# Splitting the keys of the second layer's first two query units, with the first halves issued beside the last GLU block

## The chip, the cores and the metric

The kernel runs on one core of a Trainium2 chip (trn2). The metric is the device time of one execution in microseconds (us). Before the change the median of three executions is 2244.06 us (2243.4 to 2244.54). One further execution was taken with the profiler; all rows below come from it.

## What is computed

Two identical layers are applied to `x` of 2048 rows and 448 columns. Each is multi-query attention (16 heads of 28, one shared key and value head) followed by a gated block with 1792 hidden columns, both on layer-normed input and added to `x`:

```python
q = (x @ wq).reshape(B, S, H, Dh)          # 16 heads of 28
k, v = x @ wk, x @ wv                      # one head for all
p = softmax(einsum("bhqd,bkd->bhqk", q, k) * Dh ** -0.5)
x = x + einsum("bhqk,bkd->bhqd", p, v).reshape(B, S, H * Dh) @ wo    # on layernorm(x)
x = x + (sigmoid(x @ w_gate) * (x @ w_up)) @ w_down                   # on layernorm(x)
x = the same two lines once more, with the same weights
```

## The kernel before

The program is written out by hand in one order for all engines (`manual_schedule`); every engine works through its own instructions strictly in that order, and what reaches a buffer or a result too early waits.

**Units and steps.** The 2048 query rows are 16 units of 128 rows, the 2048 keys 16 tiles of 128. A step is one unit with one key tile: four score products `s` (line 584, four heads each, 512 columns), four exponentials `P` on ScalarE (line 587), and four products with the values, `pv` (line 595, 32 columns of the array each; the trace shows two records for each, so 8 a step), which sum over the unit's 16 steps into one PSUM tile. A layer is 256 steps. `pv` runs one or two steps behind the scores, from the list `waiting`.

**Row maxima.** The exponential needs each row's maximum first. For each unit and each range of 512 keys, class `Maxima` issues groups of four products `mx` (line 549), which VectorE reduces with four instructions `mp` (line 554). The last quarter of the keys of unit 0 in layer 2 is cut finer (256, 128, 128), since those keys come last. When a unit's groups are done, `row_max` reduces them to one number per row, `fin` transposes it (`mt`, line 575), VectorE copies it (`mr`), and a DMA from GpSimd writes it as row 28 of the unit's queries `QS`, where the score product subtracts it. Only then may the unit's scores start.

**Filler.** Query projections (`qp`, line 352), the output projection (`wo`, line 695) and the gated block (`gp`, `up`, line 352; `dn`, line 784) of units that are done are cut into slices and issued between the scores (`PATHS` gives the pattern of a pair of steps, `Filler.slice` the amount). A gated (GLU) block covers two units, and 14 column tiles of 128 in 7 pairs; its tanh `th` and its `h` go through ScalarE and VectorE. `pvs`, `sums`, `rc` and `lb` (lines 599 to 669) divide a unit by its row sums through small DMAs.

**Between the layers.** Layer 2 needs all keys of layer 1's output, so after step 256 of layer 1 a `while` loop (line 1131) issues the rest of layer 1's filler in rounds of 1800 ns, and beside it those maxima of layer 2 (units 0 to 3) whose keys exist. When the last two units' gated block is through, key tiles 14 and 15 are made on the shortest path (`db`, `dct`, `dd`, `det`), unit 0's last maxima follow, and the loop over layer 2's steps starts. Its first three units have pattern `C`; their filler is only the query projections of blocks 1 to 3, the rest of the maxima of units 0 to 3 (`sparse`) and three `wo`, until the first gated block is ready near step 49.

**Buffers.** PSUM has seven tiles in rotation (tag `f`) for `s`, `mx` and all filler, and one for `pv`. A new tile waits for the readers of the tile seven allocations back.

In the text, the *passage* is the part from layer 1's last score to the first transposition of key tile 14 (1108.3 to 1200.5 us), the *closing* from there to layer 2's first score (to 1222.9 us), and the *light stretch* layer 2's units 0 to 2 (to 1350.5 us).

## Time and profile before

| | us |
|---|---|
| median of three executions | 2244.06 |
| profiled execution | 2247.71 |
| its span, first to last instruction | 2245.9 |
| TensorE busy (PE) | 2195.5 (98%) |
| VectorE busy (DVE) | 1643.7 (73%) |
| ScalarE busy (ACT) | 1552.8 (69%) |
| GpSimd busy (POOL) | 335.9 (15%) |

A timeline row gives the start, the time from the first start to the last end, engine, line, operation, tiles, shape and count. TensorE's records overlap, so what a group costs is read from its start to the start of the next row. A number in square brackets is idle time of the engine ahead of the row and what ended it.

### The profile page before, as it was taken

To read this page: it belongs to the slowest core of one execution; us is meant where nothing else is said; L and a number is where in the kernel's file an instruction comes from. 1 tells how busy PE (TensorE), PEld (TensorE's weight loads), DVE (VectorE), ACT (ScalarE), POOL (GpSimd) and SP (SyncE) were. 2 spreads that over 40 slices of the span, in tenths; PEclk is the share of its full clock that TensorE was granted. 3 is DMA by queue.
4 is the path that set the end of the run, shared out by engine and by line. 5 is a ranking of instruction groups with operands and counts; after the bars stand their busy time and mean duration, and the time that the engine had idled before them with its cause. 6 is when DMAs were issued, how large, how long until landed. Compare 5 with 4: busy or idle time off the path is not lost.

```text
span 2245.9 us, 41454 instructions
## 1 busy us (share of the span) xinstructions
PE 2195.5 (98%) x15915; PEld 1030.8 (46%) x15915; DVE 1643.7 (73%) x2905; ACT 1552.8 (69%) x2595; POOL 335.9 (15%) x590
## 2 busy tenths in 40 slices
PE   7998999999999999999999999999999999999999
PEld 3322344444544445454564324445454544445467
DVE  7888888777777787777796557777777777777222
ACT  5698777776667677676614997777676767777741
POOL 5113764101010100101012010000000000000010
PEclk9999999999999999999999999999999999999999
DMA  4333662323313232331441113323231313223233
GB/s 143 106 97 94 197 215 81 106 79 85 112 60 102 64 100 90 97 107 49 119 154 35 36 52 108 80 88 99 67 108 49 100 59 103 76 88 96 75 118 108
DMA packets 203622, 213.28 MB, mean 95 GB/s; under 512 B 135376, under 2 KB 164240, under 8 KB 203424
## 3 DMA queue, kind: packets, MB, share of 16 engines
q1 hardware_dynamic: 198080, 195.78, 29.2%
q0 software_dynamic: 5344, 14.87, 1.9%
q8 instruction: 124, 2.03, 0.4%
q14 instruction: 74, 0.61, 0.1%
HBM read 175.37 MB, written 23.59 MB: 89 GB/s over the span
## 4 chain that ended last, share of the span: by engine, by line
PE 86%; DVE 8%; ACT 2%; issue 1%; DMA 1%; SPq 1%; POOL 0%; DVEq 0%; ACTq 0%; POOLq 0%
PE pv L595 20%; PE s L584 19%; PE up L352 11%; PE dn L784 11%; PE gp L352 11%; PE mx L549 7%; DVE mp L554 6%; PE wo L695 3%; PE qp L352 2%; ACT P L587 1%; DMA wgu<-wgu_d 0%; DMA rq<-in_A_wq_dram 0%; DMA rc<-sums 0%; PE hot L916 0%; DVE sgu L131 0%
## 5 line engine op out<-in xcount | busy, mean ns | idle before, releaser
L587 ACT ACTIVATE P<-s,esc 128x512 f32<-128x512 f32 x2048 | 1297.8, 690 | 474.5 <-PE s L584 462.8
L554 DVE TENSOR_REDUCE mp<-mx 128x1 f32<-128x512 f32 x2048 | 1269.4, 682 | 389.2 <-PE mx L549 385.4
L584 PE MATMUL s<-QS,KK 96*128 96x512 f16 x2048 | 673.8, 381 | 21.3 <-DVE mp L554 14.8
L352 PEld LDWEIGHTS <-wgu 128*128 128x128 f16 x4928 | 467.6, 97 | 182.1 <-issue 42.9
L595 PE MATMUL pv<-P,VV 128*32 128x512 f32 x4096 | 510.7, 602 | 0.0
L352 PE MATMUL gp<-XT,wgu 128*128 128x256 f16 x2464 | 349.2, 272 | 2.4 <-DVE mp L554 1.7
L352 PE MATMUL up<-XT,wgu 128*128 128x256 f16 x2464 | 348.3, 272 | 0.7 <-DVE mp L554 0.7
L784 PE MATMUL dn<-WD,h 128*128 128x448 f16 x1344 | 301.0, 352 | 0.0
L584 PEld LDWEIGHTS <-KK 96*128 96x128 f16 x2048 | 189.7, 97 | 212.5 <-issue 114.5
L595 PEld LDWEIGHTS pv<-P,VV 128*32 128x32 f32 x4096 | 98.7, 108 | 244.6 <-issue 242.6
L549 PE MATMUL mx<-KK,QH 32*128 32x512 f16 x1792 | 185.3, 386 | 3.0 <-DVE mp L554 1.7
L784 PEld LDWEIGHTS <-h 128*128 128x128 f16 x1344 | 126.5, 97 | 129.4 <-issue 14.5
L549 PEld LDWEIGHTS <-QH 32*128 32x128 f16 x1792 | 46.0, 91 | 256.5 <-issue 252.7
L669 POOL TENSOR_TENSOR lb<-pvs,lb 128x512 f32<-128x512 f32 x32 | 41.1, 1284 | 739.1 <-DMA lb<-sums 619.8
L757 ACT ACTIVATE h<-th 128x512 f16<-128x512 f32 x112 | 70.3, 628 | 61.8 <-DVE th L754 61.5
L754 DVE SCALAR_TENSOR_TENSOR th<-th,up 128x512 f32<-128x512 f32 x112 | 76.2, 680 | 48.9 <-PE up L352 42.2
L306 POOL TENSOR_SCALAR rs<-mv 128x1 f32<-128x1 f32 (+1 forms) x50 | 11.2, 225 | 656.6 <-DVE mv L291 573.6
L352 PE MATMUL qp<-XT,WQ 128*128 128x512 f16 x352 | 108.3, 390 | 0.7 <-DVE mp L554 0.4
L746 ACT ACTIVATE th<-gp,gsc 128x512 f32<-128x512 f32 x112 | 76.8, 685 | 32.8 <-PE gp L352 32.6
L758 DVE SCALAR_TENSOR_TENSOR h<-th,h 128x512 f16<-128x512 f32 x112 | 79.9, 713 | 20.8 <-ACT h L757 20.8
L695 PE MATMUL wo<-WO,oT 128*128 128x448 f16 x384 | 89.7, 352 | 0.2 <-ACT P L587 0.2
L352 PEld LDWEIGHTS <-WQ 128*128 128x128 f16 x352 | 32.9, 99 | 54.9 <-issue 28.9
(151 smaller groups left out, 918.1 us busy)
## 6 DMA issues: line engine op xcount, KB each, us to landing
wgu<-wgu_d SPq DMA_DIRECT2D x224, 512.0 KB
QS<-qd SPq DMA_DIRECT2D x384, 32.0 KB
lb<-sums SPq DMA_DIRECT2D x128, 64.0 KB
xr<-in_A_x_dram SPq DMA_DIRECT2D x32, 224.0 KB
qd<-qst POOLq DMA_DIRECT2D x28, 256.0 KB, 2.7
wgu_d<-sgu POOLq DMA_DIRECT2D x14, 512.0 KB, 3.7
x2d<-x SPq DMA_DIRECT2D x16, 224.0 KB
xr<-x2d SPq DMA_DIRECT2D x16, 224.0 KB
```

The costliest lines, as they stand in the source:

```text
L352: nc.tensor.matmul(ps, a, b, start=n == 0, stop=n == 10)
L549: nc.tensor.matmul(ps[h][:, i * w:(i + 1) * w], qh[32 * h:32 * h + 32, g], KK[l][32 * h:32 * h + 32, 1, ka:kz], start=True, stop=True, til ...
L554: nc.vector.tensor_reduce(o, ps[h].rearrange("p (g k) -> p g k", g=n), axis=AX.X, op=OP.max)
L584: nc.tensor.matmul(s, KK[l][0:96, 0, kt * 128:(kt + 1) * 128], QS[l, u][:, g].rearrange("p h n -> p (h n)"), start=True, stop=True)
L587: nc.scalar.activation(p, s, AF.Exp, scale=esc)
L595: nc.tensor.matmul(v[32 * g:32 * g + 32], VV[l][:, kt], P[g], start=kt == 0, stop=kt == KT - 1, tile_position=(0, 32 * g))
L695: nc.tensor.matmul(p, v["oT"][:, a, h * 128:(h + 1) * 128], WO[:, c, h], start=n == 0, stop=n == 11)
L746: defer(lambda: nc.scalar.activation(th, gp.rearrange("p j n -> p (j n)"), AF.Tanh, scale=gsc))
L754: nc.vector.scalar_tensor_tensor(t, th, 1.0, up.rearrange("p j n -> p (j n)"), op0=OP.add, op1=OP.mult)
L757: nc.scalar.activation(h[:, 0], t, AF.Copy, scale=2.0 ** -17)
L758: defer(lambda: nc.vector.scalar_tensor_tensor(h[:, 1], t, 2.0 ** -17, h[:, 0], op0=OP.mult, op1=OP.subtract), 3)
L784: nc.tensor.matmul(p, hs[f // 2][:, a, o:o + 128], WD[:, f, c], start=n == 0, stop=n == 3 * FC - 1)
```

## The change

For units 0 and 1 of layer 2 the keys are taken in two halves of 8 tiles. The first halves have their own maxima (`part` 0) and are issued in the loop between the layers, one score product after the second and the fourth slice of a round (`ahead`), with `pv` two steps behind; 64 score products in all. Their sums are kept in SBUF as `pva`. The layer's own loop starts at step 16 of a new list of steps, with the second halves of units 0 and 1, then unit 2 and so on. The factor between the two maxima, exp of their difference, is made from both rows (`fe`), spread over the partitions by way of DRAM (`fd`, `fb`) and multiplied into `pva` on GpSimd, which also adds `pva` to the second half. Unit 1's last quarter of keys is now cut finer as unit 0's is. For space, `HB` (buffers of `h`) goes from 10 to 8, `s2` from 3 to 2, and `pvs` from 1 to 2. The core of the diff:

```diff
-    TB, WB, HB = 2, 4, 10
+    TB, WB, HB = 2, 4, 8
...
+    CUT = 8
+    def rescale(l, u):
+        if (l, u) in SCB and (l, u) in PVA:
+            nc.gpsimd.tensor_tensor(PVA[l, u], PVA[l, u], SCB.pop((l, u)), op=OP.mult)
+            scaled.add((l, u))
+
+    def halved(l, u):
+        return l == 1 and u < 2
+
+    def segments(l):
+        out = [(u, 0, CUT) for u in range(U) if halved(l, u)]
+        return out + [(u, CUT if halved(l, u) else 0, KT) for u in range(U)]
...
-        ends = [0, 512, 1024, 1536] + ([1792, 1920] if l and u == 0 else []) + [2048]
+        ends = [0, 512, 1024, 1536] + ([1792, 1920] if l and (u == 0 or halved(l, u)) else []) + [2048]
...
         def started(self):
-            return not any(a[0] == 0 for a in self.todo)
+            return not any(a[0] == 0 or halved(self.l, a[0]) for a in self.todo)
...
         def fin():
...
+            if part:
+                f = wk1.tile([16, 128], F32, tag="s2", name="fe", bufs=2)
+                nc.vector.tensor_tensor(f, r, ROW.pop((l, u)), op=OP.subtract)
+                nc.scalar.activation(f, f, AF.Exp, scale=fsc[0:16])
+                nc.sync.dma_start(fd[u % 2], f)
+                v = {}
+
+                def spread():
+                    v["b"] = wk1.tile([128, 512], F32, tag="lb", name="fb", bufs=1)
+                    for g in range(G):
+                        nc.sync.dma_start(v["b"][32 * g:32 * g + 32], fd[u % 2].rearrange("(g h) n -> g (h n)", g=G)[g:g + 1]
+                                          .to_broadcast([32, 512]))
...
+                def scale():
+                    SCB[l, u] = v["b"]
+                    rescale(l, u)
...
+                later((1, spread), (1, scale))
...
-        if kt == KT - 1:
-            o = wk1.tile([128, 512], F32, name="pvs", bufs=1)
+        if kt == z - 1 and z < KT:
+            o = PVA[l, u] = wk1.tile([128, 512], F32, name="pva")
             nc.scalar.copy(o, v)
+            rescale(l, u)
+        elif kt == z - 1:
+            o = wk1.tile([128, 512], F32, name="pvs", bufs=2)
+            nc.scalar.copy(o, v)
+            if a:
+                nc.gpsimd.tensor_tensor(o, o, PVA.pop((l, u)), op=OP.add)
             PVS[l, u] = o
...
+    def ahead(n):
+        for _ in range(n):
+            u, kt, a, z = STEPS[1][sc[0]]
+            if z == KT or ("m", 1, u, 0) not in stored:
+                return
+            if part_p == [] and len(waiting) > 1:
+                pv(*waiting.pop(0))
+            scores(1, u, kt, a, z, len(part_p), part_p)
+            if len(part_p) == G:
+                waiting.append((1, u, kt, a, z, list(part_p)))
+                part_p.clear()
+                sc[0] += 1
...
-            sparse = [i * (3 * KT - 1) // n for i in range(n)]
+            sparse = [sc[0] + i for i in range(4)]
+            sparse += [sc[0] + 5 + i * (3 * KT - 6 - sc[0]) // (n - 4) for i in range(n - 4)]
...
-        for step in range(U * KT):
-            u, kt = divmod(step, KT)
+        for step in range(sc[0] if l else 0, U * KT):
+            u, kt, lo, hi = STEPS[l][step]
...
-            for _ in range(0 if fine else 5):
+            for i in range(0 if fine else 5):
                 fill.slice(VS / 5)
+                if nx and i in (1, 3):
+                    ahead(1)
...
-                    go = n >= 2 and not fine
+                    go = (n >= 2 or halved(l + 1, a[0])) and not fine
```

Counted in the order of the instructions on TensorE, from layer 1's last score to the start of the gated work in layer 2:

| | passage before | passage now | closing before | closing now | light stretch before | light stretch now |
|---|---|---|---|---|---|---|
| `s` | 0 | 64 | 0 | 0 | 192 | 128 |
| steps of `pv` | 2 | 16 | 0 | 0 | 46 | 32 |
| groups of `mx` | 24 | 27 | 3 | 5 | 23 | 18 |
| `gp` and `up` | 436 | 436 | 0 | 0 | 0 | 0 |
| `dn` | 151 | 151 | 17 | 17 | 0 | 0 |
| `qp` | 0 | 0 | 50 | 50 | 78 | 77 |
| `wo` | 12 | 12 | 0 | 0 | 24 | 24 |

From unit 3's first step on, TensorE's order is the same but for one `qp`. Before layer 1's last score one transposition (`mt`) is added, and the maxima of layer 2 that are taken early come in another order.

On ScalarE, in the passage, gated work alone stood in a row before (`th` is the tanh, `h` its use after VectorE's product, `ktl` and `VV` the new keys and values):

```order
L746 ACTIVATE th<-gp,gsc 128x512
L379 ACTIVATE ktl_112<-kv 128x7x28
L380 ACTIVATE VV<-kv 128x28
L757 ACTIVATE h<-th 128x512
L746 ACTIVATE th<-gp,gsc 128x512
```

At the same place it now reads:

```order
L809 ACTIVATE th<-gp,gsc 128x512
L379 ACTIVATE ktl_112<-kv 128x7x28
L380 ACTIVATE VV<-kv 128x28
L641 ACTIVATE P<-s,esc 128x512 x4
L820 ACTIVATE h<-th 128x512
L641 ACTIVATE P<-s,esc 128x512 x2
L809 ACTIVATE th<-gp,gsc 128x512
```

Some six exponentials stand in each pair of `th` and `h`, two of them behind an `h`.

On VectorE, in the closing, after key tile 14 was transposed (`hl` is the last split of the layer norm, `ktl` key tile 15, `m` the row maximum of unit 0), before:

```order
L323 TENSOR_TENSOR hl<-xn,hl 128x384
L554 TENSOR_REDUCE mp<-mx 128x4 x4
L381 SCALAR_TENSOR_TENSOR ktl_112<-kv,ktl_112 128x28
L554 TENSOR_REDUCE mp<-mx 128x4 x4
L569 TENSOR_REDUCE m_16176<-mp 128x16
L570 TENSOR_SCALAR m_16177<-m_16176 128x16
L577 COPY mr<-mt 16x128
```

and now:

```order
L323 TENSOR_TENSOR hl<-xn,hl 128x384
L580 TENSOR_REDUCE mp<-mx 128x4 x8
L381 SCALAR_TENSOR_TENSOR ktl_112<-kv,ktl_112 128x28
L580 TENSOR_REDUCE mp<-mx 128x4 x4
L599 TENSOR_REDUCE m_16595<-mp 128x16
L600 TENSOR_SCALAR m_16596<-m_16595 128x16
L610 COPY mr<-mt 16x128
L614 TENSOR_TENSOR fe<-mr,mra 16x128
L580 TENSOR_REDUCE mp<-mx 128x4 x4
L599 TENSOR_REDUCE m_16632<-mp 128x16
L600 TENSOR_SCALAR m_16633<-m_16632 128x16
```

Four reductions of unit 1 now stand ahead of `ktl`, and four more with their row maximum behind unit 0's.

On TensorE, in the passage, one step's `pv` now stands alone between the gated products:

```order
L352 MATMUL up<-XT_14696,wgu 128x256
L651 MATMUL pv<-P,VV 32x512 x4
L638 LDWEIGHTS KK
L638 MATMUL s<-QS,KK 128x512
L352 LDWEIGHTS wgu
```

In the light stretch they stood, and stand, two steps in a row.

## Rows read from the trace of the kernel before

**Rows 1.** The page: busy time and share of each engine; one group of GpSimd.

```profile
PE 2195.5 (98%) x15915; PEld 1030.8 (46%) x15915; DVE 1643.7 (73%) x2905; ACT 1552.8 (69%) x2595; POOL 335.9 (15%) x590
...
L669 POOL TENSOR_TENSOR lb<-pvs,lb 128x512 f32<-128x512 f32 x32 | 41.1, 1284 | 739.1 <-DMA lb<-sums 619.8
```

**Rows 2.** Busy time by window: passage, closing, light stretch; after the colon the length.

```profile
core 0: us, PE busy (x) PEld busy (x) DVE busy (x) ACT busy (x) POOL busy (x), PEclk, DMA share, GB/s
1108.30:1200.50 92.20, 91.90 (x743) 60.18 (x741) 79.58 (x141) 17.47 (x31) 8.65 (x27) 1.00 0.38 120
1200.50:1222.90 22.40, 18.87 (x149) 8.98 (x146) 14.70 (x31) 8.20 (x17) 8.94 (x11) 0.93 0.25 76
1222.90:1350.50 127.60, 123.01 (x759) 38.97 (x758) 69.85 (x122) 119.26 (x202) 14.12 (x27) 1.00 0.14 41
```

**Rows 3.** Timeline of TensorE in the passage: gated products in a row.

```profile
1152.04 2.57 PE L352 MATMUL gp<-XT,wgu 128*128 128x256 f16 x22
1154.44 0.27 PE L352 MATMUL up<-XT,wgu 128*128 128x256 f16 x1
```

**Rows 4.** Timeline of TensorE late in layer 1: one step's `pv` alone.

```profile
1094.60 0.38 PE L584 MATMUL s<-QS,KK 96*128 96x512 f16 x1
1094.91 1.07 PE L595 MATMUL pv<-P,VV 128*32 128x512 f32 x8
1095.91 0.39 PE L549 MATMUL mx<-KK,QHB 32*128 32x512 f16 x4
```

**Rows 5.** Timeline of TensorE in the light stretch: part of one pair of steps.

```profile
1268.45 1.16 PE L584 MATMUL s<-QS,KK 96*128 96x512 f16 x4
1269.54 1.92 PE L595 MATMUL pv<-P,VV 128*32 128x512 f32 x16
1271.40 0.40 PE L549 MATMUL mx<-KK,QHB 32*128 32x512 f16 x4
1271.72 0.39 PE L584 MATMUL s<-QS,KK 96*128 96x512 f16 x1
1271.95 0.60 PE L352 MATMUL qp<-XT,WQ 128*128 128x512 f16 x2
1272.39 0.59 PE L584 MATMUL s<-QS,KK 96*128 96x512 f16 x2
```

**Rows 6.** Groups by line, light stretch: busy, mean ns, idle before and releasers.

```profile
L587 ACT ACTIVATE P<-s,esc 128x512 f32<-128x512 f32 x191 | 115.7, 702 | 13.3 <-PE s L584 12.9
L584 PE MATMUL s<-QS,KK 96*128 96x512 f16 x193 | 58.1, 379 | 4.3 <-DVE mp L554 4.0 <-ACT P L587 0.2
L554 DVE TENSOR_REDUCE mp<-mx 128x1 f32<-128x512 f32 x92 | 57.1, 684 | 46.6 <-PE mx L549 46.4
```

**Rows 7.** Waits in the passage: total us, times, longest us.

```profile
ACT h L757 <- DVE th L754: 35.2, 10, 5.0
```

**Rows 8.** Timeline of TensorE in the closing.

```profile
1215.95 0.22 PE L388 MATMUL kvt<-id,ktl 128*128 128x128 f16 x1
...
1216.69 0.41 PE L549 MATMUL mx<-KK,QHB 32*128 32x128 f16 x16 [0.24 <-ACT KK L392]
1220.14 0.28 PE L575 MATMUL mt<-id,m 128*16 128x128 f16 x1 [3.05 <-DVE m L570]
1220.35 2.74 PE L352 MATMUL qp<-XT,WQ 128*128 128x512 f16 x6
1222.88 1.10 PE L584 MATMUL s<-QS,KK 96*128 96x512 f16 x4
```

**Rows 9.** Timeline of VectorE in the closing.

```profile
1213.16 2.49 DVE L554 TENSOR_REDUCE mp<-mx 128x4 f32<-128x512 f32 x4 [0.76 <-PE mx L549]
1215.56 0.18 DVE L381 SCALAR_TENSOR_TENSOR ktl<-kv,ktl 128x28 f16<-128x28 f32 x1
1217.10 2.49 DVE L554 TENSOR_REDUCE mp<-mx 128x4 f32<-128x512 f32 x4 [1.36 <-PE mx L549]
1219.62 0.25 DVE L569 TENSOR_REDUCE m<-mp 128x16 f32<-128x96 f32 x1
```

More of the change, by code (lines that the diff above doesn't have):

```diff
@@ L496, in __init__ @@
                 lead = [(u, j) for u, j in todo if soon(u, groups_of(l, u)[j][2])]
-                lead.sort(key=lambda a: (groups_of(l, a[0])[a[1]][2] > S - 1024, a))
+                lead.sort(key=lambda a: (not halved(l, a[0]), not halved(l, a[0]) and groups_of(l, a[0])[a[1]][2] > S - 1024, a))
                 first = [a for a in todo if a[0] == 0 and a not in lead]
@@ L500, in __init__ @@
             self.todo = todo
-            self.left = {u: len(groups_of(l, u)) for u in range(U)}
+            self.left = {}
+            for a in todo:
+                p = a[0], self.part(a)
+                self.left[p] = self.left.get(p, 0) + 1
             self.mp = {}
@@ L504, in __init__, with part @@
                 load_qh(l, 0)
+        def part(self, a):
+            return int(halved(self.l, a[0]) and groups_of(self.l, a[0])[a[1]][1] >= CUT * 128)
         def need(self, a):
@@ L525, in visit @@
                 late[i][0] -= 1
-                if late[i][0] <= 0 and late[i][2] in QS:
+                if late[i][0] <= 0 and late[i][2] in QS and (not late[i][3] or ("s",) + late[i][2] in stored):
                     late.pop(i)[1]()
@@ L588, in scores, with pv @@
         P.append(p)
-    def pv(l, u, kt, P):
-        if kt == 0:
+        if kt == z - 1 and g == G - 1:
+            stored.add(("s", l, u))
+    def pv(l, u, kt, a, z, P):
+        if kt == a:
             PVS[l, u] = psv.tile([128, 512], F32, tag="v", name="pv")
@@ L1058, in interleaved_layers_kernel @@
     VS = 1800
+    STEPS, FETCH, ENDS = {}, {}, {}
+    for l in range(layers):
+        seg = segments(l)
+        STEPS[l] = [(u, kt, a, z) for u, a, z in seg for kt in range(a, z)]
+        end = {u: i for i, (u, *_) in enumerate(STEPS[l])}
+        begin = {u: min(i for i, t in enumerate(STEPS[l]) if t[0] == u) for u in range(U)}
+        FETCH[l] = {(end[u - 2] + 1 if halved(l, u - 1) or halved(l, u - 2) else begin[u - 1] + 2): u for u in range(1, U)
+                    if not halved(l, u)}
+        ENDS[l] = {i + 2: u for u, i in end.items()}
+    waiting, part_p, sc = [], [], [0]
+    def ahead(n):
+        for _ in range(n):
+            u, kt, a, z = STEPS[1][sc[0]]
+            if z == KT or ("m", 1, u, 0) not in stored:
+                return
+            if part_p == [] and len(waiting) > 1:
[5 more added lines that the diff above has]
+                sc[0] += 1
     for l in range(layers):
@@ L1061, in interleaved_layers_kernel @@
         final = l + 1 == layers
-        while late:
+        if l:
+            mx.visit()
+            while part_p:
+                ahead(1)
+        while late and not l:
             late.pop(0)[1]()
@@ L1087, in interleaved_layers_kernel @@
             single = "P" in pair[0] and "P" in pair[1]
-            for o in pair[kt % 2]:
+            for o in pair[step % 2]:
                 if o == "S":
-                    scores(l, u, kt, len(P), P)
+                    scores(l, u, kt, lo, hi, len(P), P)
                 elif o == "M":
@@ L1102, in interleaved_layers_kernel @@
                                 mxs[l + 1].step(a)
-                    if kt == 2 and u + 1 < U:
-                        load_qs(l, u + 1)
+                    if step in FETCH[l]:
+                        load_qs(l, FETCH[l][step])
+                    if not final and step == U * KT - KT + 3:
+                        load_qs(l + 1, 0)
                 elif o == "P":
@@ L1108, in interleaved_layers_kernel @@
                 elif o == "X":
-                    if u and kt == 1:
-                        b = (u - 1) // TB
-                        if (l, b) not in BLK:
-                            BLK[l, b] = Block(l, b)
-                        later(*BLK[l, b].tile(u - 1))
+                    if step in ENDS[l]:
+                        w = ENDS[l][step]
+                        if (l, w // TB) not in BLK:
+                            BLK[l, w // TB] = Block(l, w // TB)
+                        later(*BLK[l, w // TB].tile(w))
                     if l == 0:
@@ L1147, in interleaved_layers_kernel @@
                     n = 0
-            for _ in range(4 if fine else 0):
+            for i in range(4 if fine else 0):
                 fill.slice(VS / 4)
+                if nx and i % 2:
+                    ahead(1)
         if not final:
```

58 lines of the change are left out of this document (40 added, 18 removed).

## The prediction

> **What bounds the kernel now.** I read the page first, then the busy time by window around the change, then rows inside each window. The page says that TensorE is busy for 98% of the span [rows 1], but its records overlap, so what matters is how densely work follows work in each of the three stretches that the change touches [rows 2]. In the passage TensorE is busy 91.9 of 92.2 us and ScalarE only 17.5. In the light stretch ScalarE is busy 119.3 of 127.6 us. Between them lies the closing, 22.4 us in which TensorE is busy for 18.9.
>
> Whether the passage is really full is seen from pitches, start to start. The 22 `gp` take 1154.44 - 1152.04 = 2.40 us, 0.109 each [rows 3]. A score product of twice the columns takes 0.22 to 0.23 (1271.95 - 1271.72), the two `qp` behind it 0.44 together [rows 5]; so a column costs the same in the passage as elsewhere, and nothing there runs stretched. I take the passage as bound by TensorE.
>
> The light stretch is bound by ScalarE: 191 exponentials keep it busy 115.7 us, 0.606 each without the overlap, and its idle time ahead of them is 13.3 us, nearly all waiting for scores [rows 6]. Here a step costs 127.6 / 48 = 2.66 us. So 16 steps move from where ScalarE binds to where TensorE binds. The question is what the light stretch can give back, since TensorE is not idle there either.
>
> **What the passage costs.** It gains 64 scores at 0.22, that is 14.1 us. It gains 14 more steps of `pv`, each alone between other work. A lone one takes 1095.91 - 1094.91 = 1.00 us, and the score ahead of it 0.31 instead of 0.22, so 1.09 [rows 4]. In the light stretch two steps together take 1271.40 - 1269.54 = 1.86 us, or 1.95 with the same lead-in, 0.975 a step [rows 5]. Fourteen lone ones make 15.3 us, 1.6 more than in pairs. The Trainium skill, TensorEngine Tiling (Array Packing), section Key Properties, says that a change of tiling mode drains TensorE; `pv` is tiled by columns and its neighbours are not. It gives no duration, and the trace agrees by the 0.115 us above; a sum without the drain would come out 1.6 us lower.
>
> Three more groups of maxima (27 for 24) at 1271.72 - 1271.40 = 0.32 us [rows 5] add 1.0, unit 1's transposition 0.2. Together 30.6 us, all on the path, because nothing in the passage is idle to take them. VectorE has 27 groups of four reductions instead of 24, 57.1 / 92 = 0.62 us an instruction [rows 6], so 79.6 + 7.4 = 87 us in a passage of 123: it stays below, but in the first five rounds and near the end the halved units get a group in every round of about 2.6 to 3 us, each of them 2.48 us of VectorE plus the products of the GLU. I add 1 us for that, between 0 and 3. Passage: **+31.6** (30.6 to 34).
>
> **What the closing costs.** The closing is a chain. Key tile 14's maxima of unit 0 are reduced from 1213.16, `ktl` of tile 15 starts when they are through at 1215.56 [rows 9], its transposition `kvt` is at 1215.95, the last maxima at 1216.69, `mt` 3.45 us later at 1220.14, then six `qp` that take 2.53 us to the next start at 1222.88, where the scores begin [rows 8]. These six run at 0.42 us each instead of 0.22, and the granted clock of the window is 0.93 [rows 2]: TensorE had stood 3.05 us ahead of `mt`.
>
> The change puts four reductions of unit 1 ahead of `ktl`: 1215.56 - 1213.16 = +2.4 us. Then, behind unit 0's `mt`, it puts unit 1's last maxima and their `mt` ahead of the six `qp`: a second leg of 3.45 us plus 0.2 for the first `mt` and for `mr` and `fe`, +3.6. Unit 0's row is meanwhile on its way by DMA, so that adds nothing. Closing: **+6.0**. If the six `qp` should run at the full clock 1.2 us comes off; if TensorE is still at the lower clock when the scores start, up to 1 us is added: 4.7 to 7.
>
> **What the light stretch gives back.** It now has 32 steps. ScalarE loses 64 x 0.606 = 38.8 us and gains a copy of `pva` and two tiny exponentials, about 0.8: 119.3 - 38.0 = 81.3 us. TensorE's work, by the counts of its order: before, 192 scores (42.2), 23 pairs of `pv` (44.9), 23 groups of maxima (7.4), 78 `qp` (17.2), 24 `wo` of 448 columns, at 448/512 of 0.22, so 0.19 each (4.6), small things 0.5, together 116.8 of 127.6 us. Now 128 scores (28.2), 16 pairs (31.2), 18 groups (5.8), 77 `qp` (16.9), `wo` 4.6, small things 0.3: **87.0 us**. So the bound changes hands: the same query projections and most of the maxima lie in two thirds of the steps, and TensorE, not ScalarE, sets the least time. Before, the stretch was 7% over its bound (127.6 / 119.3). Ends: 87.0 with no loss, 87.0 x 1.07 = 93.1. I take 91.0, nearer the upper end, since the first four steps have a group of maxima each, so that a pair of steps there asks for eight maxima tiles of a rotation of seven. That is **-36.6** (-40.6 to -34.5).
>
> **What hides.** On GpSimd two multiplications and two additions, taken at `lb`'s 1.3 us each [rows 1], stand in a stretch where it is busy 14 of 127.6 us [rows 2]. If that cover went, the addition would delay a unit's `sums`, whose `wo` comes several steps later. SP's queue gets the two `fd` stores and eight `fb` loads behind the waiting `fe`; behind them stand unit 2's queries, not needed for 16 steps. These queries now stand ahead of unit 0's `sums`, so its reciprocal can reach VectorE late by a microsecond or two, in a stretch where VectorE is busy 69.9 of 127.6 us. The smaller `HB` and `s2` cost nothing: a block fills 7 of `h` and its `dn` all precede the next block's writes in TensorE's order; a third `th` comes two GLU pairs after the first.
>
> **The sum** is 31.6 + 6.0 - 36.6 = **+1.0 us**. It is made against the profiled execution of 2247.71 us, which is 3.65 over the median of the three shown; on the median it gives 2245.1. Its own range is 30.6 + 4.7 - 40.6 = -5.3 to 34 + 7 - 34.5 = +6.5, that is 2238.8 to 2250.6. A measurement of this kernel can tell about 0.2%, 4.5 us, from no change (2239.6 to 2248.5).
>
> **The rivals.**
>
> *Faster: the light stretch ends at TensorE's 87.0 us and unit 1's second leg hides in the closing.* The maxima of unit 1 would have to run while unit 0's row travels, so that only the 2.4 us ahead of `ktl` remain: 30.6 + 2.4 - 40.6 = -7.6, 2236.5 us. For it: TensorE's 3.05 us of standing before `mt` [rows 8] show that the closing has room. Against it: the order puts unit 1's `mt` ahead of the six `qp`. It decides if the light stretch stays under 88 us.
>
> *Slower: ScalarE's queue holds up the passage.* ScalarE works in order, and `h` waits for VectorE's product: 35.2 us in ten waits, 3.5 each, up to 5.0 [rows 7]. Today nothing is queued behind it. Now exponentials stand behind it, whose scores hold PSUM tiles, and TensorE stops when a tile of seven allocations back is not free. A round has about seven allocations and takes some 2.7 us, so of a 3.5 us wait 0.8 would show, in 11 GLU pairs 9 us: +1.0 + 9 = +10, 2254 us. Against it: much of the wait is only ScalarE being early, and with more to do it comes later. It decides if TensorE idles more than 5 us in the passage.
>
> *The passage is not full.* TensorE's weight loads are busy 60.2 of 92.2 us, 65% [rows 2]. If the halves fitted into the rest, only closing and light stretch would count: 6.0 - 36.6 = -30.6, 2213.5 us. The Trainium skill, Perfetto Trace Analysis, section Identifying the Most-Contended Engine, holds that busy time of matmuls is a poor measure and that the busy share of weight loads should be taken. The pitches [rows 3, 5] speak against such room here.
>
> That the change would not do what it says can be excluded from the order: all 64 scores stand in the passage.
>
> **How the numbers follow.** Forecast 0.53, of which 0.05 lies above 2248.5; faster rival 0.17, passage not full 0.03, slower rival 0.27. Hence faster 0.17 + 0.03 = 0.20, same 0.53 - 0.05 = 0.48, slower 0.27 + 0.05 = 0.32. The range takes in the forecast's own and reaches to the two nearer rivals: 2236.5 to 2254.
>
> **What would show it.** In the changed profile the passage should be about 124 us long with TensorE still busy throughout and ScalarE near 57 us; the closing about 28 us, with two waits of some 3 us ahead of `mt` instead of one; the light stretch about 91 us, at 2.84 a step instead of 2.66, with ScalarE no longer above 90%. A light stretch at 2.66 a step, or a passage under 120 us, would make the forecast wrong on the fast side; TensorE idling on ScalarE in the passage, on the slow side.

## The result, and the profile after

The changed kernel takes 2255.58 us, the median of four executions (2253.82 to 2262.27), beside 2244.26 for the kernel before in the same session: the ratio is 1.005, with a 95% interval of 1.0034 to 1.0065. It is slower by 11.3 us, where 1.0 us was forecast, and lies 1.6 us above the predicted range. The profiled execution is the slowest of the four: span 2260.3 us against 2245.9 before, so +14.4.

The profile after, busy time by window, with the passage, the closing and the light stretch as in [rows 2]; after the colon the length:

```profile
core 0: us, PE busy (x) PEld busy (x) DVE busy (x) ACT busy (x) POOL busy (x), PEclk, DMA share, GB/s
1106.60:1230.50 123.90, 123.37 (x939) 67.29 (x936) 88.14 (x154) 59.59 (x96) 9.26 (x28) 1.00 0.30 93
1230.50:1259.00 28.50, 20.60 (x181) 9.83 (x178) 20.75 (x44) 8.90 (x19) 9.85 (x13) 0.88 0.16 56
1259.00:1364.10 105.10, 99.21 (x561) 30.76 (x560) 56.28 (x99) 83.19 (x139) 18.51 (x31) 0.94 0.18 51
```

The passage grew from 92.2 to 123.9 us, +31.7 (predicted +31.6), with TensorE busy 123.37 of it. The closing grew from 22.4 to 28.5, +6.1 (predicted +6.0). The light stretch fell from 127.6 to 105.1 us, -22.5, where -36.6 was predicted. So 14 us are missing in one stage. Around the three, -1.7 us ahead of the passage and +0.8 behind unit 2 remain. ScalarE's 83.19 us in the light stretch are near the predicted 81.3, so the bound did change hands.

The light stretch alone is cut next at the points where the granted clock changes:

```profile
1252.00:1262.30 10.30, 6.82 (x36) 2.27 (x40) 4.17 (x12) 3.22 (x6) 2.47 (x4) 0.50 0.22 73
1262.30:1313.50 51.20, 47.81 (x295) 14.67 (x288) 31.17 (x53) 43.29 (x73) 8.62 (x9) 1.00 0.17 48
1313.50:1316.90 3.40, 3.40 (x9) 1.32 (x10) 0.00 (x0) 1.28 (x3) 0.00 (x0) 0.51 0.45 110
1316.90:1323.70 6.80, 6.13 (x37) 1.80 (x36) 4.28 (x9) 4.36 (x8) 1.55 (x6) 1.00 0.01 3
1323.70:1330.50 6.80, 6.32 (x23) 1.28 (x22) 2.19 (x4) 3.73 (x7) 0.00 (x0) 0.50 0.12 40
```

PEclk 0.50 is 1.2 GHz instead of 2.4. It holds for 10.3 us around the end of the closing, for 3.4 us from 1313.5, and for 6.8 us from 1323.7; before, the granted clock in the light stretch was 1.00 [rows 2]. Some 13.5 us of this lie in the light stretch, where work takes about twice its time (a pair's `pv` 3.64 us from 1326.12, 1.92 from 1318.64), so it costs about half of that. At 1313.48, where the second of the three begins, TensorE had just stood. Its timeline there:

```profile
1309.61 0.71 PE L575 MATMUL mx<-KK,QHB 32*128 32x512 f16 x4
...
1311.17 0.54 PE L758 MATMUL wo<-WO,oT 128*128 128x448 f16 x2
1313.48 1.68 PE L758 MATMUL wo<-WO,oT 128*128 128x448 f16 x4 [1.76 <-DVE oT L739]
```

And that of ScalarE and VectorE, as far as `oT` goes:

```profile
1308.66 0.64 ACT L738 CAST oT<-lb 128x512 f16<-128x512 f32 x1
...
1310.04 2.48 DVE L580 TENSOR_REDUCE mp<-mx 128x1 f32<-128x512 f32 x4 [1.09 <-PE mx L575]
1312.44 0.98 DVE L739 TENSOR_TENSOR oT<-lb,oT 128x512 f16<-128x512 f32 x1
```

`oT` is unit 0's attention output in two halves: ScalarE makes the high one, which is done at 1309.30, and VectorE the low one by a subtraction. Four reductions of a group of maxima stand ahead of the subtraction in VectorE's order, 2.4 us, and `wo` waits 1.76 us. In the kernel before it was the other way round: in the step of unit 0's `wo`, too, a group of maxima stood, but unit 2's transposition `mt` came ahead of it, and the call that takes its tile (`fps`) first issues what was put off, here the subtraction. VectorE in the kernel before:

```profile
1286.52 0.69 DVE L676 TENSOR_TENSOR oT<-lb,oT 128x512 f16<-128x512 f32 x1 [1.27 <-ACT oT L675]
1287.38 0.21 DVE L577 COPY mr<-mt 16x128 f16<-16x128 f16 x1 [0.17 <-PE mt L575]
1287.65 2.48 DVE L554 TENSOR_REDUCE mp<-mx 128x1 f32<-128x512 f32 x4
```

The third thing to see is a pair of steps with two groups of maxima (a dense pair, below), at 2.4 GHz:

```profile
1268.11 1.92 PE L651 MATMUL pv<-P,VV 128*32 128x512 f32 x16
1269.97 0.40 PE L575 MATMUL mx<-KK,QHB 32*128 32x512 f16 x4
1270.29 0.39 PE L638 MATMUL s<-QS,KK 96*128 96x512 f16 x1
...
1271.17 0.38 PE L638 MATMUL s<-QS,KK 96*128 96x512 f16 x1
1271.73 0.39 PE L575 MATMUL mx<-KK,QHB 32*128 32x512 f16 x2 [0.18 <-DVE mp L580]
1272.33 0.57 PE L575 MATMUL mx<-KK,QHB 32*128 32x512 f16 x2 [0.21 <-DVE mp L580]
1272.93 0.38 PE L638 MATMUL s<-QS,KK 96*128 96x512 f16 x1
```

The first group is through in 0.32 us (1269.97 to 1270.29). The second waits for PSUM tiles that VectorE is still reducing, and the next score starts 1.76 us after the last one (1272.93 - 1271.17). Eight scores, a pair of steps, took 7.17 us here, where pairs with one group take 5.1 to 5.7. The changed kernel has dense pairs at steps 16/17, 18/19 and 34/35; before, the groups stood in even steps alone and no pair had two. The longest stretch at 1.2 GHz within the light stretch, from 1323.69, begins behind the pair 34/35:

```profile
1320.50 0.40 PE L575 MATMUL mx<-KK,QHB 32*128 32x512 f16 x4
...
1322.86 0.37 PE L575 MATMUL mx<-KK,QHB 32*128 32x512 f16 x1 [0.21 <-DVE mp L580]
1323.16 0.68 PE L638 MATMUL s<-QS,KK 96*128 96x512 f16 x2
1324.33 1.86 PE L638 MATMUL s<-QS,KK 96*128 96x512 f16 x4 [0.48 <-ACT P L641]
```

### The profile page after: what moved, and what is told of

Read it like the earlier page. It is cut to its first block, busy times and chain, and to the rows that moved or that the text cites. A ratio compares the mean times of both kernels' runs of the same rounds, so it can differ in the third digit from the quotient of the medians.

```text
span 2260.3 us, 41560 instructions
## 1 busy us (share of the span) xinstructions
PE 2205.2 (98%) x15949; PEld 1030.4 (46%) x15949; DVE 1643.7 (73%) x2914; ACT 1558.8 (69%) x2599; POOL 341.3 (15%) x596
## 3 DMA queue, kind: packets, MB, share of 16 engines
q8 instruction: 125, 2.05, 0.4%
## 4 chain that ended last, share of the span: by engine, by line
PE 85%; DVE 8%; ACT 3%; issue 1%; DMA 1%; POOL 0%; SPq 0%; ACTq 0%; DVEq 0%; POOLq 0%
PE pv L651 20%; PE s L638 19%; PE dn L847 11%; PE up L352 11%; PE gp L352 11%; PE mx L575 7%; DVE mp L580 6%; PE wo L758 3%; PE qp L352 2%; ACT P L641 1%; DMA rc<-sums 0%; DVE sgu L131 0%; DMA rq<-in_A_wq_dram 0%; DMA rd<-in_B_w_down_dram 0%; PE hot L979 0%
## 5 line engine op out<-in xcount | busy, mean ns | idle before, releaser
L580 DVE TENSOR_REDUCE mp<-mx 128x1 f32<-128x512 f32 (+1 forms) x2048 | 1269.3, 683 | 395.1 <-PE mx L575 391.3
L638 PE MATMUL s<-QS,KK 96*128 96x512 f16 x2048 | 682.4, 382 | 20.1 <-DVE mp L580 10.2
L306 POOL TENSOR_SCALAR rs<-mv 128x1 f32<-128x1 f32 (+1 forms) x50 | 11.3, 225 | 682.8 <-DVE mv L291 589.8
L352 PE MATMUL qp<-XT,WQ 128*128 128x512 f16 x352 | 105.1, 387 | 0.8 <-DVE mp L580 0.4
L758 PE MATMUL wo<-WO,oT 128*128 128x448 f16 x384 | 91.3, 356 | 2.9 <-DVE oT L739 2.4
```

The lines of the kernel that those rows point to most:

```text
L352: nc.tensor.matmul(ps, a, b, start=n == 0, stop=n == 10)
L580: nc.vector.tensor_reduce(o, ps[h].rearrange("p (g k) -> p g k", g=n), axis=AX.X, op=OP.max)
L638: nc.tensor.matmul(s, KK[l][0:96, 0, kt * 128:(kt + 1) * 128], QS[l, u][:, g].rearrange("p h n -> p (h n)"), start=True, stop=True)
L758: nc.tensor.matmul(p, v["oT"][:, a, h * 128:(h + 1) * 128], WO[:, c, h], start=n == 0, stop=n == 11)
```

## The experiments

The theory that the profile suggests: the light stretch would take about 91 us, but stops (waits of TensorE) that the order itself makes, of `wo` and in the dense pairs, and the lower clock behind stops, add the rest. Rivals: TensorE has more work there than my 87.0 us; the late `sums` behind unit 2's queries; the buffers. Eighteen runs tell them apart. The table gives each one's stages in its profiled execution (us), the granted clock in its light stretch, and the medians and ratios to the kernel before of the same session. The passage is counted here from the start of layer 1's last score, 0.3 us earlier than in the windows above.

| run | passage | closing | light | PEclk | median | ratio, interval |
|---|---|---|---|---|---|---|
| before | 92.5 | 22.4 | 127.6 | 1.00 | 2244.3 to 2245.6 | |
| changed | 124.2 | 28.5 | 105.0 | 0.94 | 2255.58 | 1.0050 (1.0034 to 1.0065) |
| g1_after_again | 124.3 | 28.5 | 101.0 | 0.98 | 2259.96 | 1.0072 (1.0057 to 1.0086) |
| e1_even | 124.3 | 28.5 | 98.7 | 0.98 | 2256.53 | 1.0048 (1.0035 to 1.0061) |
| e2_odd | 124.2 | 28.4 | 106.4 | 0.97 | 2264.49 | 1.0088 (1.0075 to 1.0101) |
| e3_hot | 124.2 | 27.2 | 99.0 | 1.00 | 2256.39 | 1.0047 (1.0031 to 1.0064) |
| e4_u1 | 124.2 | 24.6 | 111.2 | 0.93 | 2262.59 | 1.0078 (1.0065 to 1.0091) |
| f1_calm_hot | 124.2 | 27.2 | 91.2 | 1.00 | 2248.16 | 1.0008 (0.9999 to 1.0017) |
| f2_u1_calm_hot | 124.2 | 24.3 | 95.1 | 1.00 | 2269.80 | 1.0103 (1.0090 to 1.0117) |
| f3_before_hot | 92.5 | 22.1 | 127.5 | 1.00 | 2244.44 | 0.9993 (0.9984 to 1.0002) |
| f4_one_unit | 108.6 | 22.2 | 118.0 | 0.99 | 2253.00 | 1.0033 (1.0021 to 1.0046) |
| g2_calm | 124.3 | 28.5 | 92.3 | 0.99 | 2248.40 | 1.0016 (1.0007 to 1.0025) |
| g3_row_late | 124.3 | 24.3 | 91.3 | 1.00 | 2243.26 | 0.9994 (0.9985 to 1.0003) |
| g4_pairs | 125.1 | 24.3 | 91.3 | 1.00 | 2244.63 | 0.9998 (0.9988 to 1.0008) |
| h1_wo_only | 124.3 | 28.5 | 99.4 | 0.95 | 2253.55 | 1.0040 (1.0027 to 1.0052) |
| h2_mt_only | 124.2 | 28.5 | 93.4 | 1.00 | 2252.06 | 1.0032 (1.0020 to 1.0045) |
| h3_dense_only | 124.3 | 28.5 | 96.8 | 1.00 | 2254.32 | 1.0040 (1.0027 to 1.0052) |
| h4_hold | 124.2 | 23.0 | 92.2 | 1.00 | 2243.57 | 0.9990 (0.9981 to 0.9999) |
| i1_buffers | 92.5 | 22.1 | 127.7 | 1.00 | 2246.66 | 1.0005 (0.9996 to 1.0013) |
| i2_hold_again | 124.3 | 23.1 | 92.2 | 1.00 | 2243.11 | 0.9993 (0.9984 to 1.0001) |

**The changed kernel again.** No edit.

> The changed kernel once more, on the same chip as the three below. 2253 to 2258; passage to light stretch (from layer 1's last score to unit 3's first) 257 us or a little less, with stops of wo and of the dense pairs, and half clock behind the closing and behind at least one of them, not always at the same place.

Closing and stop of `wo` (1.77 us) recur to 0.1 us; the light stretch takes 101.0 us, with 3.4 us at 1.2 GHz in its middle instead of 10.2 (3.4 and 6.8). No lower clock follows the stop of `wo` this time; the 3.4 us begin at 1320.4, behind the pair 34/35 again. The median is above the 2258 that I expected. Executions of this kernel lie between 2253.8 and 2263.0, and the higher their time the lower, by and large, their mean clock (0.996 to 0.992). Over some 2258 us, 0.004 of the clock is 9 us, so most of the spread can be where and how often the clock falls, not in the light stretch alone.

**The clock.** Idle products ("hot" ones, whose result nobody uses) stand ahead of `mt` in e3_hot (of units 0 and 1) and f3_before_hot (unit 0, kernel before):

```diff
             stored.add(("m", l, u, part))
+            if part:
+                w = fps([128, 512], F32, "hot")
+                for _ in range(12):
+                    nc.tensor.matmul(w, id16, id16.rearrange("p (o j) -> p o j", o=1).to_broadcast([128, 4, 128]),
+                                     start=True, stop=True)
```

> Twelve idle products of 512 columns (2.6 us, output unused, so added work) stand ahead of each of the two last transpositions mt, where TensorE waits 3.05 us. Theory 'clock': TensorE then does not fall to half clock behind the waits; the six qp take 1.4 us less, the first 7 us of the light stretch are at full clock: 4 to 6 us off 2255.6, 2250 to 2251.5. Theory 'rotation': only the qp gain, 1.4 us, 2254; the dense pairs still take 7 us with the clock at 1.0.

> The kernel before with the twelve idle products ahead of unit 0's mt. It had 3.4 us at half clock behind that wait, which cost 1.7 us. Theory 'clock': 1 to 2 us faster than before, closing about 21 us instead of 22.4. Rival 'the clock falls a little later instead': same time, half clock elsewhere in the profile.

In e3_hot's profile there is no 1.2 GHz from the passage to unit 3; the closing is 1.3 us shorter and the light stretch 6.0 us, in the same order of work:

```profile
1257.60:1356.70 99.10, 93.20 (x561) 29.68 (x560) 56.26 (x99) 83.04 (x139) 18.93 (x31) 1.00 0.20 55
```

Six of the 14 us in the changed kernel's first profile are thus the clock; in its second it is 2.0 (101.0 against 99.0). But the stop of `wo` (1.76 us) and the dense pairs are still there, and the median did not fall, against both theories: six executions lie between 2250.5 (mean clock 0.998) and 2261.4 (0.993). So what hot products ahead of two waits give is not kept in every execution. In the kernel before they bought 0.3 us of the closing instead of the 1.7 that 3.4 us at 1.2 GHz had cost: at the full clock the first score waits for its row instead. TensorE in f3_before_hot:

```profile
1218.86 0.22 PE L580 MATMUL mt<-id,m 128*16 128x128 f16 x1 [0.35 <-DVE m L570]
1219.02 1.47 PE L352 MATMUL qp<-XT,WQ 128*128 128x512 f16 x6
1221.33 1.04 PE L589 MATMUL s<-QS,KK 96*128 96x512 f16 x4 [0.84 <-DMA QS<-mr]
```

**Where the maxima stand.** e1_even and e2_odd change only the list of steps that get a group; g2_calm also moves the groups off the steps of `oT` and lets unit 2's `mt` come a step later; f1_calm_hot is g2_calm with e3_hot's products. Sixteen groups instead of 18 lie in the stretch in all four; the other two, 0.6 us, follow later.

```diff
-            n = sum(a[0] < 4 for a in mx.todo) + 4
-            sparse = [sc[0] + i for i in range(4)]
-            sparse += [sc[0] + 5 + i * (3 * KT - 6 - sc[0]) // (n - 4) for i in range(n - 4)]
+            sparse = [16, 18, 20, 22, 24, 26, 28, 30, 33, 34, 36, 38, 41, 42, 44, 46]   # g2_calm
...
-        late.append([4 if l and u == 3 else LT, fin, (l, u), part])
+        late.append([4 if l and u == 3 else 2 if l and u == 2 else LT, fin, (l, u), part])
```

> The maxima of the light stretch are spread evenly, one group in every even step, instead of four in the first four steps and further neighbours at steps 21/22 and 34/35. Against the changed kernel (2255.6 us). Theory 'rotation': a pair of steps with two groups asks for eight maxima tiles and stands on the reductions (7.2 us a pair where others take 5.4 to 5.7), four such pairs or so, 1.6 us each: about 6 us off, 2249 to 2250, light stretch about 98 us. Theory 'clock': the excess is TensorE's half clock after the closing's two waits, and the pairs are slow for that alone: 0 to 2 us off, 2254 to 2256.

> As e1_even, but one group in every odd step, where the slice that issues VectorE's subtraction for oT stands ahead of the group instead of behind it. Theory 'queue': the 1.8 us in which wo waits for oT, and the 3.4 us at half clock behind it, come from the reductions ahead of oT in VectorE's queue: 2 to 3.5 us better than e1_even, 2246 to 2248, no wait of wo above 0.3 us. Theory 'late sums' (unit 2's queries ahead of unit 0's sums on SP's queue make oT late, as my prediction named it): same as e1_even, wo still waits for oT.

> As e3_hot, and in the light stretch no pair of steps has two groups of maxima, none stands in the two steps whose oT would queue behind it, and unit 2's mt comes a step later. Theory 'work' (TensorE's own work there is 92.8 us, not my 87.0; stops and half clock are the rest): the 6 us of stops shrink to 1 to 3, light stretch 94 to 96 us, no half clock in it, 2247 to 2250 us where the clock holds. Rival 'sum right' (87.0 of work, the rest waits that the placement makes): light stretch at or under 91 us, 2244 or less.

> f1_calm_hot without the idle products: only the placement of the maxima (no dense pair, none ahead of oT) and unit 2's mt a step later. Theory 'stops' (most of the 14 us that my light stretch was short by are stops and the half clock behind them in the stretch itself): light stretch 94 to 95 us, of which 3 are the half clock that the closing leaves behind; closing 28.5 as before; 2250 to 2251. Rival 'clock from the closing' (its two waits bring the half clock that then lasts): light stretch 98 us or more, 2254 or more, and only the idle products make the placement worth something.

e1_even takes the dense pairs away and makes a new stop: TensorE's idle time in it is 3.8 us ahead of `wo` (two) and 1.84 ahead of unit 2's `mt`, whose row maxima now stand behind four reductions. Its profiled light stretch is 98.7 us, as 'rotation' said, but its median did not move; 'clock' gets that. e2_odd answers the question on `oT`: no `wo` waits, although unit 2's queries still stand ahead of the `sums`. It was the queue of VectorE, not SP's; ScalarE's half of `oT`, done at 1309.30 in the changed kernel before the reductions began, says the same. As a whole it missed: the scores now wait for ScalarE in 20 places (8.4 us), with 6.8 us at 1.2 GHz behind some of them, and unit 3 waits 1.4 us for its row.

g2_calm removes all three kinds, the dense pairs, the stops of `wo` and this one of `mt`. Its light stretch is 92.3 us, 2 us less than 'stops' expected, and its median 11.6 us below the changed kernel's in the same session. The closing's two waits are unchanged, so 'clock from the closing' falls. With the products as well, f1_calm_hot comes to 91.2 us, the figure of the prediction. Both of f1's theories fell: the stretch is below 94, and above 91 by a hair. TensorE in f1_calm_hot's light stretch:

```profile
1253.30:1344.40 91.10, 88.57 (x552) 29.36 (x551) 50.94 (x91) 82.06 (x139) 18.77 (x30) 1.00 0.21 60
```

88.57 busy, so my 87.0 was 1.6 short, although two groups of maxima (0.6 us) fewer lie in it. The rival 'more work' is worth no more than 2.2 us.

**One stop at a time.** Each is g2_calm with one of its parts undone, or the changed kernel with one part done: e1_even's list with the later `mt` (h1), g2_calm's list without it (h2), and the neighbours kept but off `oT`'s step (h3):

```diff
+            sparse = [16, 17, 18, 19, 21, 22, 24, 26, 28, 30, 33, 34, 36, 38, 39, 41, 43, 45]   # h3_dense_only
```

> e1_even with unit 2's mt a step later: no dense pair, no wait of mt in the light stretch, but two steps where oT stands behind four reductions and wo waits 1.8 to 2.1 us. Theory 'one stop is enough' (a stop of TensorE of about 1.8 us is paid and half clock may follow): light stretch 96 to 97 us, 3.8 over g2_calm's 92.3 for the two stops, and half clock behind at least one of them in some runs; 2251 to 2254. Rival 'dense pairs did it': as g2_calm but for at most 1 us, 2248 to 2249.

> g2_calm without the later mt of unit 2: one wait of 1.84 us ahead of mt, where the row maxima stand behind four reductions. Theory 'one stop is enough': light stretch 94 to 96 us, 2249.5 to 2252. Rival: the wait is taken from a later one, as g2_calm.

> The changed kernel with its neighbours at 16 to 19, 21/22 and 38/39 kept, but no group in the step of oT. Theory 'dense pairs': 1.6 us for each of two to four dense pairs, 3 to 5 over g2_calm: light stretch 96 to 98; together with the half clock from the closing, which then meets the slow pairs, 2251 to 2254. Rival 'the wo stop did it': as g2_calm, 2248 to 2249.5.

The light stretches of g2_calm and h3_dense_only:

```profile
1256.40:1348.60 92.20, 89.67 (x552) 29.56 (x551) 50.93 (x91) 82.05 (x139) 18.54 (x30) 0.99 0.20 59
```

```profile
1258.10:1354.90 96.80, 92.45 (x560) 29.74 (x559) 56.04 (x99) 83.11 (x139) 18.43 (x31) 1.00 0.19 56
```

Against g2_calm's 92.3 us: two stops of `wo` +7.1, of which 3.8 are the waits and the rest two stretches of 3.4 us at 1.2 GHz behind them, which cost half their length; the one of `mt` +1.1; the dense pairs +4.5. Medians +5.2, +3.7 and +5.9, from one session to the next. The three do not start alike: the closing leaves 2.3 us at 1.2 GHz in g2_calm's light stretch, 0.8 in h2_mt_only's and next to none in h3_dense_only's. Taken at the full clock, by half of these, `mt` cost 1.9 us, its whole wait, and the dense pairs 5.6, of which 0.6 are the two groups more that h3_dense_only has. So each stop by itself costs time, as 'one stop is enough' and 'dense pairs' said, and the rivals of all three fall, though the light stretch came out above what I had expected of h1_wo_only (96 to 97) and below what I had of h2_mt_only (94 to 96). That it is the seven PSUM tiles that make a dense pair slow was not tried with another number of tiles; it rests on the waits for `mp`. The first stop in h1_wo_only, on TensorE's timeline:

```profile
1311.03 1.67 PE L758 MATMUL wo<-WO,oT 128*128 128x448 f16 x4 [1.77 <-DVE oT L739]
```

**The closing.** e4_u1 leaves unit 1's last group and its row to the light stretch; f2_u1_calm_hot does so in the calm order; g3_row_late moves only the row; h4_hold also holds the group over key tile 14 back until unit 0's row is through, and puts the light stretch's first group a step later. The core of the last two:

```diff
-        late.append([4 if l and u == 3 else LT, fin, (l, u), part])
+        late.append([4 if l and (u == 3 or u == 1 and part) else 2 if l and u == 2 else LT, fin, (l, u), part])
...
-            a = a or next((a for a in r if halved(self.l, a[0])), None)
+            a = a or next((a for a in r if halved(self.l, a[0]) and (self.need(a) < S - 128 or KVD[self.l] == NT)), None)
```

> Unit 1's last group of maxima and its row are taken out of the closing and done in the light stretch's first step. Both theories: the closing loses the second leg, 28.5 to 24.5 us or so. Theory 'clock': with one wait of 3 us instead of two the half clock is as short as in the kernel before (3.4 us), another 3 us off: 2248 to 2249. Theory 'rotation': the light stretch takes the group too, 0.3 to 1.5 us more: 2252 to 2253.

> As f1_calm_hot, and unit 1's last group of maxima and its row are done in the light stretch instead of the closing (idle products only ahead of unit 0's mt). e4_u1 came out slower with a closing 3.9 us shorter, because its mt there stood 1.87 us and half clock followed. Theory 'stops bring half clock': with mt a step later the gain of the closing stays: 3 us better than f1, 2244 to 2247. Rival 'the second leg is paid anywhere': same as f1 or slower.

> f1_calm_hot with unit 1's last row (its mt and what follows) taken out of the closing into the light stretch's third step; its maxima stay where they are, and idle products stand only ahead of unit 0's mt. Theory 'second leg': the closing loses 3.65 of its 6.0 us, about 24 us long with full clock, and nothing in the light stretch waits for the row, so 3 us off f1: 2244 to 2246, the same as before. Rival 'the leg only hid another wait' (unit 0's row of queries, on its way by DMA, holds the first score): 1 us off f1 at most.

> g3_row_late with unit 1's maxima over key tile 14 also held back until unit 0's row is through, so that nothing of unit 1 stands on VectorE ahead of ktl, and the first group of the light stretch half a step later. My term 'four reductions ahead of ktl, +2.4' says: closing 2.4 us shorter than g3_row_late's, with kvt no longer waiting 1.3 us; light stretch within 0.5: 2240 to 2242, 0.1 to 0.2% faster than before. Rival 'the closing is a chain of other things' (tile 15's transpositions, copies, the row's way by DMA): 1.3 us at most; or the eight maxima in a row bring a stop at the start of the light stretch, no gain.

> h4_hold once more. If its gain is real, the ratio is again 0.998 to 0.9995; closing about 23 us, light stretch about 92 us, no half clock between the passage and unit 3. If it was the draw of executions, 0.9995 to 1.001.

e4_u1 shortens the closing by 3.9 us and loses 6.2 in the light stretch: two stops of `mt` (3.7 us), one of `wo` (2.1), and the clock at 0.93. It came out slower than either theory had said. f2 is a failure of my own edit: 16 groups where 19 were due leave the later units' rows late, and behind the light stretch scores wait 11 times for `QS<-mr`, 11.5 us in all. g3_row_late: the closing falls by 2.9 us against f1_calm_hot, the light stretch stays, and the ratio falls from 1.0008 to 0.9994, 3 us: 'second leg' holds. h4_hold: closing 1.3 us less again, not 2.4, which is what its rival said, and the median 1.6 us above the 2242 that I had hoped for. TensorE at its end:

```profile
1249.71 0.22 PE L610 MATMUL mt<-id,m 128*16 128x128 f16 x1 [0.35 <-DVE m L600]
1249.87 0.58 PE L575 MATMUL mx<-KK,QHB 32*128 32x128 f16 x19
1251.23 0.38 PE L575 MATMUL mx<-KK,QHB 32*128 32x128 f16 x13 [0.78 <-DVE mp L580]
1251.82 1.46 PE L352 MATMUL qp<-XT,WQ 128*128 128x512 f16 x6 [0.22 <-DVE mp L580]
1253.12 0.88 PE L643 MATMUL s<-QS,KK 96*128 96x512 f16 x3
```

`kvt` no longer waits (1.30 us in the changed kernel), but unit 1's two groups now follow each other, and TensorE waits 0.78 and 0.22 us for their reductions. This version is 12 to 17 us faster than the changed kernel (2243.57 and 2243.11 beside 2255.58 and 2259.96) and about 0.1% faster than the kernel before; in one of two sessions the interval takes in 1, so that much is at the edge of what these runs tell. From layer 1's last score to unit 3's first it takes 239.5 us, the kernel before 242.5; of these 3.0 us, 1.3 and 1.6 (in its two profiles) go back behind unit 3's first score, where the two groups that were put off follow.

**Half the change, pairs, buffers.** `halved` for unit 0 alone (a second line takes unit 1, now whole, out of the list that fetches queries within the layer); the passage's `pv` two steps at a time; the kernel before with only `HB` 8, `s2` 2 and `pvs` 2.

```diff
-        return l == 1 and u < 2
+        return l == 1 and u < 1
```

```diff
-            if part_p == [] and len(waiting) > 1:
+            while part_p == [] and len(waiting) > 1:
                 pv(*waiting.pop(0))
+                pv(*waiting.pop(0))
```

> Only unit 0 takes its keys in two halves; unit 1 stays whole, 8 steps instead of 16 move. Theory 'idle' (moved work costs TensorE the same in both places, the gain is bounded by TensorE's 4.6 us of idle time in the light stretch before): passage +16, closing +2.4, light stretch 127.6 - 16 - 3 = about 108, 2244 to 2248. My prediction's own arithmetic (ScalarE's share falls, TensorE's sum is 102): light stretch 102 to 109, sum between -7 and 0, 2237 to 2244.

> g3_row_late with the passage's pv two steps at a time. My lone pv cost 0.115 us a step more than in pairs, 1.6 us for fourteen: passage 1.4 to 1.6 us shorter, 2243 to 2245. Rival: the second of a pair waits for its last exponential on ScalarE, up to 0.6 us in seven pairs, so the passage is as long or longer.

> The kernel before with the change's buffers alone (HB 8 for 10, s2 2 for 3, pvs 2 for 1). My prediction: nothing, within 1 us of the kernel before. Rival: part of the 11 us lies here, layer 1 longer by some us because h or th is waited for: 2247 or more.

f4_one_unit: passage +16.1, closing -0.2 (nothing of unit 1 comes finer, so there is no second leg; I had expected +2.4), light stretch -9.6, that is 118.0 us where 108 was the first expectation and 109 the most that the second allowed. Three of its pairs are dense as well (7.26, 7.16 and 6.76 us), which is about half of what is missing; the rest is not assigned. g4_pairs: passage 0.8 us longer, not shorter. The records show its rival at work: five of the seven pairs take 1.86 us from their first `pv` to the next score, where two lone steps take 2.00, but two take 2.79 and 3.32, because the weight loads of `pv` wait there for the last exponentials. Waits of weight loads in this passage:

```profile
PEld pv L656 <- ACT P L646: 1.9, 4, 0.8
```

i1_buffers: no difference that can be measured, and layer 1 up to its last score takes 1017.9 us, before 1019.1.

## Why the prediction was wrong, point by point

- **Bounds.** Right. The passage is TensorE's (123.37 of 123.9), and after the change TensorE binds the light stretch, ScalarE no longer.
- **Passage +31.6.** Measured +31.7. Added up from start to start in the two traces, the scores bring 14.3 us (priced 14.1), and `pv` with the longer lead-in on the gated products ahead of it 15.5 (priced 15.3). Of its parts only `pv` was tried by itself. A pair that nothing delays is 0.14 us shorter than two lone steps, so lone ones do cost more; but two of the seven pairs waited for ScalarE and lost 2.4 us. The rule that I cited, the Trainium skill, TensorEngine Tiling (Array Packing), section Key Properties (changing the tiling mode drains TensorE), is neither shown nor refuted by that.
- **Closing +6.0.** Measured +6.1, with the two waits of 3.05 and 3.06 us ahead of `mt` as told. Taken away on the chip, the second leg gave 2.9 us (priced 3.6) and the four reductions ahead of `ktl` 1.3 (priced 2.4), both beside hot products. The other 1.9 us have no term in the 6.0: 1.0 is the clock (hot products shorten the closing by 1.3 us, before by 0.3), and 0.9 is what h4_hold's closing still has over f3_before_hot's. That the sum fits is in part luck.
- **Light stretch -36.6: the step that failed.** "I take 91.0, nearer the upper end, since the first four steps have a group of maxima each", I wrote. Measured 105.0 and 101.0. The 91 us exist: f1_calm_hot takes 91.2, without any of the stops. What the 4.0 us of loss in that sentence had to pay was mis-sized, and two of the causes were put at nothing. Dense pairs with their two groups more cost 5.6 us (h3_dense_only against f1_calm_hot, three such pairs, both at the full clock), the stop of `wo` 1.8: with f1's 91.2 that makes 98.6, where e3_hot, which has both at the full clock, took 99.0. The rest of the 105.0, 6.0 us, is TensorE at 1.2 GHz; in the second profile it is 2.0.
- **The clock.** "If TensorE is still at the lower clock when the scores start, up to 1 us is added", I wrote, in the closing, and for the light stretch nothing. The rows of before had one wait of 3.05 us and 3.4 us at the lower clock behind it. I doubled the wait, and did not ask what the second would do to the clock; the answer was 10.3 us in a row. In the light stretch the lower clock came behind stops of its own. (The 4.7 that I gave as the closing's least should be 4.8, 6.0 less 1.2; nothing hangs on it.)
- **What hides.** I had the right chain in view, unit 0's sums up to `wo`, and the wrong queue. SP's order (unit 2's queries ahead of `sums`) stayed in e2_odd and g2_calm, and no `wo` waited. What delayed it was a group's reductions ahead of `oT` on VectorE, which I had called not busy. Nor was this a wait that something had covered before: in the kernel before, the group of that step (24 then, 32 now) stood behind `oT` on VectorE, and no `wo` could wait for it. The change moved unit 2's `mt`, which had stood between, away from that step, and with it the order. A comparison of VectorE's order around `oT`, such as I made for the closing, would have shown it before any run.
- **The sum as a whole.** TensorE's idle time in the light stretch before was 127.60 - 123.01 = 4.6 us [rows 2], and moved work costs TensorE as much in the passage. So by the records no order could win much more than 5 us there, while the closing's chain got 6 longer. My own terms said the same (31.6 - 36.6 = -5.0), and h4_hold ends near it: -3.0.
- **Rivals.** None came. TensorE did not idle on ScalarE in the passage, and the second leg did not hide. The passage was full: every product put there lengthened it, though weight loads were busy for only 67.29 of 123.90 us, 54%. By the share of weight loads, which the Trainium skill, Perfetto Trace Analysis, section Identifying the Most-Contended Engine, names as one of two measures of TensorE's headroom, there was room; here the pitches told it better. The slower side came by a mechanism that stood in the text only as details; my chance for slower was 0.32, most of it (0.27) placed on ScalarE's queue in the passage.

## What to carry to other kernels

When a change moves work between stages, go through the new order of every in-order engine, not only of the one that binds, for short operations that TensorE waits for: a group of reductions that stood behind such an operation may now stand ahead of it. Where TensorE binds, such a wait is paid in full, and may be paid a second time at the lower clock. Before asking how much moved work costs at each end, read the bound engine's idle time in the stage that is relieved: here it was 4.6 us, and the best order won 3.0 up to unit 3. Judge a stage by what it takes when nothing stops it, and then list the stops.

## What the runs showed of the hardware

- Stops of 1.45 to 2.23 us, well below the closing's 3.05, were followed by 3.4 or 6.8 us at 1.2 GHz, begun by the stop's end or up to 1.4 us after it, in the changed kernel (1.76 us), in h1_wo_only (1.77 and 2.06), in e1_even (the one of 2.06), in e4_u1 (1.87, 1.84 and 2.05), in e2_odd (1.45, unit 3's row) and in f2_u1_calm_hot (2.23, the same); in e1_even (1.77 and 1.84), e3_hot (1.76), g1_after_again (1.77) and h2_mt_only (1.84) the same kind of stop was not.
- Nor did it take a single stop as long: behind the dense pair 34/35, where no wait of TensorE shows more than 0.5 us, the lower clock came in both profiles of the changed kernel (6.8 and 3.4 us); behind the dense pairs of e3_hot and h3_dense_only it did not. In e2_odd 6.8 us of it began at 1296.3, amid waits for ScalarE of at most 0.78 us each.
- What such stretches cost shows in the windows of h1_wo_only, where two follow the stops, and of h2_mt_only, where none does (light stretch; PEclk 0.95 and 1.00):

```profile
1260.10:1359.50 99.40, 93.62 (x552) 30.53 (x551) 51.25 (x91) 81.94 (x139) 18.27 (x30) 0.95 0.19 54
```

```profile
1258.90:1352.30 93.40, 89.31 (x552) 29.34 (x551) 50.85 (x91) 82.18 (x139) 18.39 (x30) 1.00 0.20 58
```

- The same program can take a different course in each execution by this: the changed kernel's light stretch took 105.0 and 101.0 us in two profiles of one order of work. Its nine executions spread over 9 us, but so can those of the kernel before (11 us in 27, in one session), so the spread by itself says little on this stage.
- At 2.4 GHz a wait can hide in the records: TensorE's idle time in the light stretch was 4.4 us with dense pairs (h3_dense_only, 96.80 - 92.45) and 2.5 without (g2_calm, 92.20 - 89.67), 1.8 apart, while the stretches, at the full clock and without the work of two groups, lie 5.0 apart.
